# Value blocks of the later four heads are loaded at attention steps 5 and 8 instead of 2 and 5

## The chip, the cores and the metric

The kernel runs on one core of a Trainium2 chip. The metric is the device time of one execution in microseconds, lower is better.

## The reference

Two blocks follow each other: a sparse attention over a window and over block summaries, and a low-rank token mix with a two-layer network behind it. There are 4 batches, 8 heads, 768 tokens and a head size of 64; the network is 512 to 2048 to 512 wide.

```python
k_sum = k.reshape(B, H, nb, block, D).max(axis=3)      # block = 32
v_sum = v.reshape(B, H, nb, block, D).mean(axis=3)
scores_l = scale * q @ k.T                             # kept where |i - j| < 16
scores_s = scale * einsum(q, k_sum) + log(block)
a = softmax(concat([masked scores_l, scores_s]))
x = a @ concat([v, v_sum])                             # then heads side by side
u = x + (x.T @ U @ V).T
out = u + relu(u @ w_ch1) @ w_ch2
```

The change concerns `v_sum`: the mean of each block of 32 value rows, which the attention needs beside the values.

## The kernel before

Matmul operands are split into a high and a low part (ScalarE rounds, VectorE or POOL subtracts), so that each product takes three passes. The first batch's network also makes the split weights and stores the unsplit ones and some of their sums to DRAM. For each of the batches 2 to 4 (`cur`) two phases follow in the loop at the end of `body`:

- the **up phase** (`up_phase`), with the weights in eight groups of four blocks; it yields after every product of six matmuls (a *piece*), 54 pieces in the loop;
- the **down phase** (`down_phase`), sixteen blocks of weights.

Beside these matmuls, the attention of the next batch (`ahead`) is worked off in 32 steps of `later_step`. Step i belongs to head i // 3. The first 15 steps (0 to 14, `FIRST_STEPS`) are spread evenly over the pieces 4 to 54 of the up phase, so that step 2 stands at piece 10, step 4 at 17, step 5 at 20, step 7 at 27, step 8 at 30 and step 10 at 37. The others go into the down phase. So the up phase of batch 2 carries the first half of batch 3's attention, and the up phase of batch 3 that of batch 4.

Each engine works in the order in which the program is written out. Several orders matter here.

- **SyncE issues all DMAs.** Among them are the weights kept in DRAM (`whole`, in `fetch_weight`, called by `tick` four pieces after a block is used up by its split), keys `kt`, queries `qz`, values `vt`, the turned squares of the attention weights (`there`, then `at`), the outputs (`out_t`) and the value blocks (`stage`, from `vn`).
- **Weights.** `prepare` splits a fetched block: ScalarE casts the high part (L186), POOL subtracts (L187).
- **Value sums.** `load_vsum(st, g, i)` loads two blocks of 128 x 512 floats, 256 KB each, for half i of head group g (g = 1 are the later four heads). `add_vsum(st, g, i)` is a generator of seven or eight small POOL adds, put on a list `slow`; `drip` takes one of them per piece. After the second half POOL scales the sum (L275), and `value_summaries` (L340) copies it on ScalarE behind each head's values. For g = 1 the first such copy is that of step 16, at the beginning of the down phase.
- **Bank copies.** The product `third` of the up phase ends in a ScalarE copy (L1262), after which TensorE may use the bank again.

The blocks `stage`, the outputs `o` and some temporaries take turns in one pool of eight buffers.

Of the kernel before, what the change touches and what calls it, by code (L numbers as in the profile page):

```python
# [86 lines left out]
def body(ctx: ExitStack, tc, q0, q1, k, v, vn, uv, w1, w2, mask, ident, rep, out):  # L87
# [29 lines left out]
    def hidden_place(k, dt=F32):  # L117
        return wt.tile([P, 4 * NH], dt, name="place", tag=f"h{k}")
# [98 lines left out]
    def load_qk(st, h):  # L217
        load_k(st, h)
        load_q(st, h)
# [7 lines left out]
    def load_v(st, h):  # L227
        vt = kv.tile([KC, 2, NU, DV], F32, name="vt")
        nc.sync.dma_start(out=vt[:W, 0], in_=v[st.b, 0, :, h])
        nc.sync.dma_start(out=vt[NB:, 1], in_=v[st.b, 1, :, h])  # L230
        st.vt[h] = [vt[:, i] for i in range(2)]
# [7 lines left out]
    def load_vsum(st, g, i):  # L239

        parts = 2
        n = BLOCK * D // (2 * parts)
        spare = None
        if st.b == 1 or st.b == 2 and g == 0:
            spare = hidden_place(2 + i)
        st.vn[g, i] = []
        for j in range(parts):
            if spare is not None:
                t = spare[:, j * n : (j + 1) * n]
            else:  # L250
                t = mo.tile([P, DM], F32, name="stage", tag="val", bufs=VALS)[:, :n]
            k = i * parts + j
            nc.sync.dma_start(out=t, in_=vn[st.b, g, :, k * n : (k + 1) * n])
            st.vn[g, i].append(t)

    def add_vsum(st, g, i):

        for j, t in enumerate(st.vn.pop((g, i))):
            n = t.shape[1] // 2
            while n > D:  # L260
                nc.gpsimd.tensor_tensor(t[:, :n], t[:, :n], t[:, n : 2 * n], ALU.add)
                yield
                n //= 2
            if i == 0 and j == 0:
                st.vsum[g] = small.tile([P, DV], F32, name="vsum")
                nc.gpsimd.memset(st.vsum[g][:, D:], 1.0)
                nc.gpsimd.tensor_tensor(st.vsum[g][:, :D], t[:, :D], t[:, D : 2 * D], ALU.add)
                yield
            else:
                nc.gpsimd.tensor_tensor(t[:, :D], t[:, :D], t[:, D : 2 * D], ALU.add)  # L270
                yield
                nc.gpsimd.tensor_tensor(st.vsum[g][:, :D], st.vsum[g][:, :D], t[:, :D], ALU.add)
                yield
        if i == 1:
            nc.gpsimd.tensor_scalar_mul(st.vsum[g][:, :D], st.vsum[g][:, :D], 1.0 / BLOCK)  # L275
# [33 lines left out]
    def key_maxima(st, h):  # L309
        block_maxima(st, h)  # L310

        spread_maxima(st, h, nc.scalar.copy if st.b == 1 else nc.vector.tensor_copy)
# [25 lines left out]
    def value_summaries(st, h, i, copy):  # L338
        r0, r = 32 * (h % 4), (W, 0)[i]
        copy(  # L340
            st.vt[h][i][r : r + NB],
            st.vsum[h // 4][r0 : r0 + NB].unsqueeze(1).broadcast_to([NB, NU, DV]),
        )
# [19 lines left out]
    def scores_by_subtiles(st, h):  # L363

        st.neg[h] = small.tile([P, NU], F32, name="neg")
        qt, kt = st.qt[h].rearrange("p u q -> p (u q)"), st.kt[h]
        ps = [bank("ps_s") for _ in range(2)]  # L370
        for i in range(3):
            for s in range(2):
                for a in range(2):
                    j = ORDER.index(2 * i + a)
                    q0, k0 = 64 + j * P + 64 * s, (j // 2) * KP + (j % 2) * KC
                    r, c = 64 * ((s + a) % 2), 64 * s
                    nc.tensor.matmul(  # L377
                        ps[a][c : c + 64, i * KC : (i + 1) * KC],
                        qt[r : r + 64, q0 : q0 + 64],
                        kt[r : r + 64, k0 : k0 + KC],  # L380
                        start=True,
                        stop=True,
                        tile_position=(r, c),
                    )
        for a in range(2):
            st.ps_s[h, a] = ps[a]
# [5 lines left out]
    def exponentials(st, h, a):  # L392
        ps = st.ps_s.pop((h, a))
        if h not in st.e and st.b == 0:
            st.e[h] = e0[h % 4]
        elif h not in st.e:
            st.e[h] = att.tile([P, NU * KC + PAD], F32, name="e", bufs=1)
            if st.b > 1:
                nc.gpsimd.memset(st.e[h][:, NU * KC :], 0.0)
        e = tiles_of(st.e[h])  # L400
        for i, u in enumerate(tiles_in_bank(st, a)):
            m = 0 if u == 0 else (3 if u == NU - 1 else 1 + u % 2)
            nc.vector.tensor_tensor_reduce(  # L403
                out=e[:, u, :],
                in0=ps[:, i * KC : (i + 1) * KC],
                in1=mask_sb[:, m, :],
                scale=-SCALE,
                scalar=BIG,
                op0=ALU.add,
                op1=ALU.min,  # L410
                accum_out=st.neg[h][:, u : u + 1],
            )
            nc.scalar.activation(  # L413
                e[:, u, :],
                e[:, u, :],
                AF.Exp,
                bias=st.neg[h][:, u : u + 1],
                scale=-1.0,
            )
# [16 lines left out]
    def send_squares(st, h):  # L436
        there = dram.tile([P, 4, NU * 32], F32, name="there")
        nc.sync.dma_start(out=there, in_=st.at[h].rearrange("p j u q -> p j (u q)"))
        st.at[h] = there

    def fetch_squares(st, h):

        there = st.at[h].rearrange("(i k) j c -> j k i c", k=32)
        at = st.at[h] = att.tile([P, 4, NU, 32], F32, name="at", tag="at", bufs=1)
        for j in range(4):
            nc.sync.dma_start(
                out=at[32 * j : 32 * j + 32].rearrange("k i u q -> k i (u q)"), in_=there[j]
            )
# [39 lines left out]
    def square_values(st, h):  # L488

        at, vt = st.at.pop(h), st.vt[h]  # L490
        ps = st.psx[h] = bank("ps_x")
        for u in range(NU):
            for i in range(4):
                nc.tensor.matmul(  # L494
                    ps[32 * i : 32 * i + 32, u * DV : (u + 1) * DV],
                    at[:KC, i, u],
                    vt[u % 2][:, (u // 2) * 2 + (i // 2 + u) % 2],
                    start=True,
                    stop=True,
                    tile_position=(0, 32 * i),  # L500
                )

    def normalise(st, h):
        ps = st.psx.pop(h)[:, : NU * DV].rearrange("p (u d) -> p u d", d=DV)
        s = small.tile([P, NU], F32, name="sum")
        nc.vector.tensor_scalar_add(s, ps[:, :, D], 1e-9)
        nc.vector.reciprocal(s, s)
        nc.vector.tensor_tensor(
            st.x[:, :, h * D : (h + 1) * D],
            ps[:, :, :D],  # L510
            s.unsqueeze(2).broadcast_to([P, NU, D]),
            ALU.mult,
        )
# [19 lines left out]
    slow = []  # L533
# [10 lines left out]
    def later_step(st, i):  # L544

        h, a = divmod(i, 3)
        if a == 0:  # L550
            if 1 <= h <= H:
                send_squares(st, h - 1)
            if 2 <= h <= H + 1:
                fetch_squares(st, h - 2)
            if h < H:
                scores_by_subtiles(st, h)
                exponentials(st, h, 0)
            if 3 <= h <= H:
                load_v(st, h - 1)
        elif a == 1:  # L560
            if h < H:
                exponentials(st, h, 1)
            if h + 1 < H:
                key_maxima(st, h + 1)
            if 1 <= h <= H:
                for t in range(2):
                    value_summaries(st, h - 1, t, nc.scalar.copy)
        else:
            if h + 2 < H:
                load_qk(st, h + 2)  # L570
            if h == 2:
                st.x = mo.tile([P, NU, DM], F32, name="x")
            if 2 <= h <= H + 1:
                square_values(st, h - 2)
                normalise(st, h - 2)
            if h < H:
                turn_squares(st, h)
        if i in (2, 5):
            load_vsum(st, 1, i // 5)
        if i in (4, 7):  # L580
            slow.append(add_vsum(st, 1, i // 7))
        if i in MIX:
            mix(st, 2 * MIX.index(i))
        if i - 1 in MIX:
            mix_back(st, 2 * MIX.index(i - 1))
# [389 lines left out]
    st = sts[0]  # L975
# [465 lines left out]
```

## Time and profile before

| | |
|---|---|
| timed runs of before | 666.3, 666.86, 669.9 us; median 666.86 |
| profiled execution | 668.33 us, of it the span 666.5 us |
| mean granted TensorE clock | 0.997 |
| busy: VectorE, ScalarE, POOL | 371.7, 358.5, 361.0 us |
| up phase of batch 2 / 3 / 4 | from about 226 / 381 / 532 us |
| down phase of batch 2 / 3 / 4 | from about 298 / 449 / 595 us |
| DMA: read from HBM, written | 91.10 MB, 24.12 MB |

Lines of the profile name an engine, the source line, the operation and the tiles that it writes and reads. In the timeline the first two columns are the start and the duration in us, and the bracket at the end is the idle time ahead of it with what ended that. Rows of a list of waits give the total, the number and the longest. Rows on DMAs give the size of one and the us from issue to landing.

### The profile page before, as it was taken

The numbers are of one execution on the slowest core, as the hardware profiler recorded it, in microseconds if no ns is written. First come the engines' busy times: TensorE is split into PE (matmuls) and PEld (weight loads), VectorE is DVE, ScalarE is ACT, GpSimd is POOL, SyncE is SP. The second block draws the span as 40 slices with busy tenths as digits, with TensorE's granted clock in tenths as the row PEclk, the third lists the DMA queues.
The fourth block names the chain that finished last, engine by engine and source line by source line (L and its number), as shares of the span: only waits on it lengthen the run. The fifth ranks groups of instructions, "written<-read, shape, count | busy, mean of one in ns | idle before, by whom it ended". The sixth has DMA issues, their size and how long they took to land.

```text
span 666.5 us, 14015 instructions
## 1 busy us (share of the span) xinstructions
PE 640.6 (96%) x5232; PEld 562.6 (84%) x5232; DVE 371.7 (56%) x1006; ACT 358.5 (54%) x803; POOL 361.0 (54%) x402
## 2 busy tenths in 40 slices
PE   5899999999999898999999999999999999999997
PEld 4789889988888797997787899997787899998885
DVE  5578866668777763567544645566644521232223
ACT  4666666655553555765453467665453365553322
POOL 5424975965577676762336487662334375653310
PEclk9999999999999998999999999999999999999999
DMA  8997497766774268787457059787441055331002
GB/s 219 228 367 239 135 315 240 230 173 195 227 225 163 72 178 265 213 251 203 147 142 205 25 171 325 228 247 204 138 143 59 24 171 178 112 126 64 32 1 94
DMA packets 76420, 116.13 MB, mean 174 GB/s; under 512 B 6976, under 2 KB 52928, under 8 KB 76352
## 3 DMA queue, kind: packets, MB, share of 16 engines
q1 hardware_dynamic: 76352, 115.24, 57.1%
q8 instruction: 41, 0.67, 0.4%
q14 instruction: 27, 0.22, 0.1%
HBM read 91.10 MB, written 24.12 MB: 173 GB/s over the span
## 4 chain that ended last, share of the span: by engine, by line
PE 83%; DVE 4%; DMA 4%; ACT 3%; POOL 2%; issue 2%; SPq 1%; ACTq 0%; POOLq 0%; DVEq 0%
PE acc L1288 30%; PE ps_h L1203 25%; PE acc L942 7%; PE ps_h L920 7%; PE ps_x L494 3%; PE ps_s L354 2%; PE ps_o L739 2%; PE ps_s L377 2%; DMA place<-in_uv 1%; DMA place<-in_q 1%; PE ps_m L666 1%; DMA whole<-up 1%; PE ps_t L463 1%; PE ps_x L480 1%; POOL place L187 1%
## 5 line engine op out<-in xcount | busy, mean ns | idle before, releaser
L187 POOL TENSOR_TENSOR parts<-whole,parts 128x512 fp32r<-128x512 f32 (+1 forms) x144 | 180.5, 1262 | 160.4 <-ACT parts L186 151.3
L1288 PE MATMUL acc<-parts,gh 128*128 128x512 f32 x576 | 192.3, 399 | 0.0
L1203 PE MATMUL ps_h<-op,parts 128*128 128x384 f32 x1008 | 187.5, 340 | 3.2 <-ACT place L1262 2.9
L1203 PEld LDWEIGHTS ps_h<-op,parts 128*128 128x128 f32 x1008 | 175.4, 189 | 6.2 <-ACT place L1262 3.2
L1288 PEld LDWEIGHTS acc<-parts,gh 128*128 128x128 f32 x576 | 108.1, 188 | 23.7 <-issue 1.7
L1288 PE MATMUL acc<-parts,gl 128*128 128x512 f32 x288 | 112.6, 391 | 0.0
L1273 DVE SCALAR_TENSOR_TENSOR gl<-place,gh 128x768 fp32r<-128x768 f32 x48 | 56.2, 1171 | 97.1 <-ACT gh L1272 97.1
L186 ACT CAST parts<-whole 128x512 fp32r<-128x512 f32 (+1 forms) x144 | 83.6, 584 | 9.9 <-DMA whole<-up 8.2
L920 PE MATMUL ps_h<-place 128*128 128x384 f32 x384 | 74.5, 342 | 0.0
L1272 ACT ACTIVATE gh<-place 128x768 fp32r<-128x768 f32 x48 | 40.6, 846 | 60.0 <-PE acc L1288 59.9
L413 ACT ACTIVATE e<-e,neg 128x120 f32<-128x120 f32 x144 | 46.3, 386 | 47.4 <-DVE neg L403 45.7
L942 PE MATMUL acc<-place,gh 128*128 128x512 f32 x192 | 68.4, 410 | 1.3 <-POOL place L187 1.3
L920 PEld LDWEIGHTS ps_h<-place 128*128 128x128 f32 x384 | 65.9, 188 | 1.0 <-DVE place L721 0.3
L162 POOL TENSOR_SCALAR val<-place 128x512 f32<-128x512 f32 (+1 forms) x30 | 47.0, 1582 | 30.8 <-ACT place L149 14.2
L1288 PEld LDWEIGHTS acc<-parts,gl 128*128 128x128 f32 x288 | 54.2, 188 | 9.9 <-DVE gl L1273 0.3
L187 POOL TENSOR_TENSOR place<-val,place 128x512 fp32r<-128x512 f32 x29 | 39.4, 1378 | 18.6 <-ACT place L186 15.3
L187 POOL TENSOR_TENSOR op<-tmp,op 128x384 fp32r<-128x384 f32 x24 | 25.4, 1067 | 39.2 <-ACT op L186 39.2
L942 PEld LDWEIGHTS acc<-place,gh 128*128 128x128 f32 x192 | 35.6, 188 | 10.5 <-POOL place L187 3.2
L403 DVE CUSTOM_DVE_ANT_0 e<-ps_s,mask_sb 128x120 f32<-128x120 f32 x144 | 32.5, 276 | 13.3 <-PE ps_s L377 8.5
L942 PE MATMUL acc<-place,gl 128*128 128x512 f32 x96 | 37.6, 392 | 0.0
L932 ACT ACTIVATE gh<-ps_h 128x384 fp32r<-128x384 f32 x32 | 15.7, 490 | 36.4 <-PE ps_h L920 36.0
L1263 DVE TENSOR_TENSOR place<-place,ps_h 128x384 f32<-128x384 f32 x24 | 13.3, 553 | 38.4 <-ACT place L1262 38.3
(124 smaller groups left out, 858.8 us busy)
## 6 DMA issues: line engine op xcount, KB each, us to landing
place<-in_w SPq DMA_DIRECT2D x32, 512.0 KB, 5.6
whole<-up SPq DMA_DIRECT2D x24, 512.0 KB, 3.9
whole<-down SPq DMA_DIRECT2D x24, 512.0 KB, 3.7
whole<-up SPq DMA_DIRECT2D x24, 384.0 KB, 3.3
vt<-in_v SPq DMA_DIRECT2D x48, 146.2 KB, 4.1
kt<-in_k SPq DMA_DIRECT2D x24, 288.0 KB, 5.4
out_t<-o SPq DMA_DIRECT2D x32, 192.0 KB, 2.2
there<-squares SPq DMA_DIRECT2D x16, 384.0 KB, 4.4
```

The costliest lines, as they stand in the source:

```text
L162: nc.gpsimd.tensor_scalar(f32(bits), f32(hi), 0.0, None, ALU.mult)
L186: nc.scalar.copy(hi, val)
L187: engine.tensor_tensor(lo, val, f32(hi), ALU.subtract)
L403: nc.vector.tensor_tensor_reduce(out=e[:, u, :], in0=ps[:, i * KC : (i + 1) * KC], in1=mask_sb[:, m, :], scale=-SCALE, scalar=BIG, op0=ALU ...
L413: nc.scalar.activation(e[:, u, :], e[:, u, :], AF.Exp, bias=st.neg[h][:, u : u + 1], scale=-1.0,)
L494: nc.tensor.matmul(ps[32 * i : 32 * i + 32, u * DV : (u + 1) * DV], at[:KC, i, u], vt[u % 2][:, (u // 2) * 2 + (i // 2 + u) % 2], start=Tr ...
L920: nc.tensor.matmul(ps[:, :NH], w_split[0, f][:, c % 2, part_w, c // 2], ut[:, c, :], start=(n == 0), stop=(n == 3 * NC - 1),)
L942: nc.tensor.matmul(acc[t], gt[:, sl], w_split[1, f][:, part_w], start=(first and j == 0), stop=(last and j == 2),)
L1203: nc.tensor.matmul(ps, a[:, sa, i], b[:, sb, i], start=(first and n == 0), stop=(n == 5), skip_group_check=not first,)
L1272: nc.scalar.activation(gh, h, AF.Relu)
L1273: nc.vector.scalar_tensor_tensor(gl, h, 0.0, f32(gh), ALU.max, ALU.subtract)
L1288: nc.tensor.matmul(acc[t], gt[:, sl], w[:, part_w], start=(f == 0 and j == 0), stop=(f == NF - 1 and j == 2),)
```

## The change

In `later_step`, the loads of the later four heads' value blocks go from the steps 2 and 5 to the steps 5 and 8, and the adds from the steps 4 and 7 to the steps 7 and 10.

```diff
-        if i in (2, 5):
-            load_vsum(st, 1, i // 5)
-        if i in (4, 7):
-            slow.append(add_vsum(st, 1, i // 7))
+        if i in (5, 8):
+            load_vsum(st, 1, i // 8)
+        if i in (7, 10):
+            slow.append(add_vsum(st, 1, i // 10))
```

TensorE, VectorE and ScalarE keep their order. On SyncE, this is the place of step 2 in the up phase of batch 2: keys, queries, value blocks, then kept weights (`whole`), the turned squares, and weights again. Before:

```order
L208 DMA kt<-in_k 128x3x192
L214 DMA qz_84<-in_q 64x3x128
L215 DMA qz_84<-in_q 64x4x128
L253 DMA stage<-in_vn 128x512 x2
L877 DMA whole<-up_109 128x768
L438 DMA there<-squares 128x768
L877 DMA whole<-up_110 128x1024
```

And now:

```order
L208 DMA kt<-in_k 128x3x192
L214 DMA qz_84<-in_q 64x3x128
L215 DMA qz_84<-in_q 64x4x128
L877 DMA whole<-up_109 128x768
L438 DMA there<-squares 128x768
L877 DMA whole<-up_110 128x1024
```

The two value blocks no longer stand between the queries and the weights. Step 5 has two value blocks in both orders. The other place on SyncE is step 8 of the same up phase; here the difference, with the fetches of the turned squares (`at`) at its end:

```order
 L214 DMA qz_84<-in_q 64x3x128
 L215 DMA qz_84<-in_q 64x4x128
+L253 DMA stage<-in_vn 128x512 x2
 L877 DMA whole<-up_112 128x768
 L438 DMA there<-squares 128x768
```

Two value blocks now stand ahead of the weights and the squares of that step. The up phase of batch 3 has the same two differences; there an output (`out_t`) stood between the value blocks and the weights at step 2.

On POOL, the first adds (L261 to L272) of the up phase of batch 2 stood among the splits of weights (L187) like this before:

```order
L187 TENSOR_TENSOR parts<-whole,parts 128x2x256 x2
L261 TENSOR_TENSOR stage<-stage 128x256
L187 TENSOR_TENSOR parts<-whole,parts 128x256
L261 TENSOR_TENSOR stage<-stage 128x128
L187 TENSOR_TENSOR parts<-whole,parts 128x2x256
L266 MEMSET vsum 128x1
L267 TENSOR_TENSOR vsum<-stage 128x64
```

And now, from the same first row on:

```order
L187 TENSOR_TENSOR parts<-whole,parts 128x2x256 x2
L187 TENSOR_TENSOR parts<-whole,parts 128x256
L187 TENSOR_TENSOR parts<-whole,parts 128x2x256 x3
L399 MEMSET e 128x8
L187 TENSOR_TENSOR parts<-whole,parts 128x256
L187 TENSOR_TENSOR parts<-whole,parts 128x2x256
L261 TENSOR_TENSOR stage<-stage 128x256
L261 TENSOR_TENSOR stage<-stage 128x128
```

Six splits now come ahead of the first add; the scaling of the finished sum (L275) stands five splits later than before.

## The prediction

> **What bounds the kernel now.** I began with the page's first table: TensorE is the bound, so a change pays only where it removes idle or slow time of that engine.
>
> ```profile
> PE 640.6 (96%) x5232; PEld 562.6 (84%) x5232; DVE 371.7 (56%) x1006; ACT 358.5 (54%) x803; POOL 361.0 (54%) x402
> ```
>
> Next the waits of TensorE inside the two stretches that the change touches. The first list is from 223 to 381 us (batch 2 in its up phase, batch 3 in attention), the second from 381 to 533 us (batches 3 and 4).
>
> ```profile
> PE ps_h L1203 <- ACT place L1262: 2.9, 1, 2.9
> ...
> PE ps_h L1203 <- POOL parts L187: 0.3, 1, 0.3
> ```
>
> So there is one wait of size after the start, of 2.87 us, and all but none in the second up phase. The timeline of TensorE shows where it lies, and that the 24 matmuls behind it take longer than the 24 of a later piece.
>
> ```profile
> 246.50 6.54 PE L1203 MATMUL ps_h<-op,parts 128*128 128x384 f32 x36
> 255.92 6.02 PE L1203 MATMUL ps_h<-op,parts 128*128 128x384 f32 x24 [2.87 <-ACT place L1262]
> 269.93 4.45 PE L1203 MATMUL ps_h<-op,parts 128*128 128x384 f32 x24
> ```
>
> Idle runs from 253.05 to 255.92. Then 24 matmuls take 6.02 us and not 4.45, which is 1.57 us more. The windows say why: in 256 to 261 us the granted clock was 0.66, which is 5 x 0.34 = 1.70 us lost. (In the rows below, the columns behind the window are its length, then busy time of PE, PEld, DVE, ACT and POOL, the granted clock, the DMA share and GB/s.)
>
> ```profile
> 250.00:253.00 3.00, 3.00 (x18) 2.72 (x16) 1.33 (x8) 0.06 (x1) 0.26 (x1) 1.00 1.02 404
> 253.00:256.00 3.00, 0.13 (x2) 0.09 (x1) 0.10 (x1) 2.96 (x8) 1.94 (x2) 1.00 1.10 340
> 256.00:261.00 5.00, 5.00 (x20) 5.00 (x21) 1.99 (x4) 2.60 (x7) 4.54 (x8) 0.66 0.85 256
> ```
>
> I take 1.6 us, between the two readings. The place costs 2.87 + 1.6 = 4.5 us in this execution. What ended the wait stands on ScalarE:
>
> ```profile
> 248.26 0.61 ACT L186 CAST parts<-whole 128x512 fp32r<-128x512 f32 x1
> 252.94 0.62 ACT L186 CAST parts<-whole 128x512 fp32r<-128x512 f32 x1 [4.06 <-DMA whole<-up]
> 253.46 0.96 ACT L413 ACTIVATE e<-e,neg 128x120 f32<-128x120 f32 x3
> 254.45 1.05 ACT L340 COPY vt<-vsum 24x390 f32<-24x390 f32 x2
> 255.40 0.46 ACT L1262 COPY place<-ps_h 128x384 f32<-128x384 f32 x1
> ```
>
> ScalarE stood for 4.06 us on the landing of one block of kept up weights. Three exponentials, two summary copies and the copy of L1262, for which TensorE waits, are queued behind that cast. From the landing (252.86) to TensorE's restart pass 3.06 us, so a landing by 253.05 - 3.06 = 249.99 would cost TensorE nothing. SyncE's issues show what that block queued behind; the second fence gives, for the issues at 243.99, 244.64, 245.28 (the pair's second) and 245.81, the us to landing in the last column.
>
> ```profile
> 243.99 0.60 SPq L215 DMA_DIRECT2D qz<-in_q  x1
> 244.64 1.08 SPq L253 DMA_DIRECT2D stage<-in_vn  x2
> 245.81 0.38 SPq L877 DMA_DIRECT2D whole<-up  x1
> ```
>
> ```profile
> qz<-in_q SPq DMA_DIRECT2D x1, 128.0 KB, 3.6
> stage<-in_vn SPq DMA_DIRECT2D x1, 256.0 KB, 5.0
> 245.28 0.43 SPq L253 DMA_DIRECT2D stage<-in_vn  x1
> stage<-in_vn SPq DMA_DIRECT2D x1, 256.0 KB, 5.8
> whole<-up SPq DMA_DIRECT2D x1, 384.0 KB, 7.0
> ```
>
> The queries landed at about 247.6, the value blocks at 249.6 and 251.1, the weights at 252.86. The two value blocks (512 KB) stand just ahead of the weights, and they are what the change takes from there.
>
> **The change, part by part.** No instruction is added or removed; two DMA issues and 7 to 9 small POOL adds move, once per value half, twice per batch, in the up phases of batches 2 and 3.
>
> *The first pair of loads leaves step 2.* The weights are then issued at 244.64 instead of 245.81, in the first value block's place. That block landed 5.0 us after this issue. The weights carry 128 KB more, 0.3 us at the 404 GB/s of the row 250 to 253, so they land by 244.64 + 5.0 + 0.3 = 249.95. The early end: behind the queries (247.6) with 384 KB at 404 GB/s (0.97 us) gives 248.6. I take 249.7, near the late end, since that is what a block in this place did. The limit is 249.99, so the wait goes, with 0.3 us in hand, and the clock loss goes with it. Is ScalarE late for another reason? The last row maximum that its exponentials need is ready at 250.08:
>
> ```profile
> 250.00 0.08 DVE L403 DVE_READ_ACCUMULATOR2_ANT neg<- 128x1 f32 x1
> ```
>
> From there follow one exponential (0.32), the copies (1.05) and L1262 (0.46): 251.9, over a microsecond ahead of 253.05. So only the landing can hold TensorE there. Bounds for this term: 4.5 us gone at most, and 2.9 at least (first rival).
>
> The next batch is a second witness. There the pair stands one issue further ahead of the same weights, and no wait of TensorE results:
>
> ```profile
> 399.06 0.38 SPq L877 DMA_DIRECT2D whole<-up  x1
> whole<-up SPq DMA_DIRECT2D x1, 384.0 KB, 6.1
> 405.15 0.62 ACT L186 CAST parts<-whole 128x512 fp32r<-128x512 f32 x1 [0.26 <-DMA whole<-up]
> 401.70 2.35 PE L1203 MATMUL ps_h<-op,parts 128*128 128x384 f32 x12
> 404.13 8.58 PE L1203 MATMUL ps_h<-op,parts 128*128 128x384 f32 x48
> ```
>
> The 37th matmul of this up piece, which needs the same L1262, begins about 404.13 + 24 x 0.18 = 408.4. A landing 3.3 us ahead sufficed there; the one I expect, 3.35 ahead of 253.05, is alike. It also says that the later weight loads keep up when TensorE does not pause, with a value pair still at step 5 as now. In batch 3's up phase the change therefore gains nothing: 0.
>
> *Step 5 keeps a pair* (the first, no longer the second). Its queue has 512 KB less ahead of it.
>
> *Step 8 gets a pair*, behind the queries issued at 267.18. The next weights are issued only at 271.78, since they wait for POOL:
>
> ```profile
> 267.18 0.60 SPq L215 DMA_DIRECT2D qz<-in_q  x1
> qz<-in_q SPq DMA_DIRECT2D x1, 128.0 KB, 4.8
> 271.78 0.33 SPq L877 DMA_DIRECT2D whole<-up  x1
> 272.68 2.21 SPq L446 DMA_DIRECT2D at<-there  x4
> 281.56 0.89 PE L494 MATMUL ps_x<-vt,at 120*32 120x65 f32 x48
> DMA to landing us min/median/max: 3.7/4.4/5.0
> ```
>
> Two issues (1.08 us) fit into the 4 us that SyncE stands there, so nothing is issued later. The pair's transfer, 1.3 us at 404 GB/s or 3.5 us (from 247.6 to 251.1, over which the old pair landed), is over by 275.5, since those queries landed 4.8 us after their issue, at 272.0. The first to feel it are the four fetches of the turned squares: issued until 274.9, landed by 279.3, needed by TensorE at 281.56, with 2.3 us to spare. Cost: 0. If that cover is gone it is the last rival.
>
> *The adds on POOL.* They run two groups later, beside other splits. POOL was busy 19.0 of 24 us in the old stretch and 7.85 of 14 in the one behind it, which takes the second group:
>
> ```profile
> 254.00:278.00 24.00, 22.08 (x197) 20.92 (x197) 10.62 (x37) 15.27 (x38) 19.00 (x30) 0.93 0.77 220
> 278.00:292.00 14.00, 14.00 (x143) 13.25 (x143) 7.95 (x35) 9.50 (x23) 7.85 (x8) 1.00 0.87 245
> 277.50 0.37 POOL L275 TENSOR_SCALAR vsum<-vsum 128x64 f32<-128x64 f32 x1
> 303.93 1.05 ACT L340 COPY vt<-vsum 24x390 f32<-24x390 f32 x2
> ```
>
> The sum is ready at 277.87 and first used at 303.93. Ten pieces later (six matmuls each, 6.54/6 = 1.1 us, and some attention between) it is ready near 290: over 10 us in hand. Splits wait on a single add of at most 0.73 us at a time, as now. Cost: 0, bounds -0.3 (a split freed earlier near 255) and +0.3.
>
> **Sum.** 668.33 (span 666.5 and 1.83 around it) - 4.5 = **663.8 us**. The median of the timed runs of before, 666.86, lies 1.5 under the profiled execution. Either two of three timed runs had the wait without the slow clock (668.33 - 1.6 = 666.7 fits two of them); then they fall by 2.9, to 663.4 to 664.0. Or they had both, and end at 661.8 to 662.4. I give the first reading six parts in ten, so that 663.8 is the forecast, 0.46% under the median. What a measurement of this kernel can tell from no change is about 0.5%, 663.5 us: the forecast sits at this edge.
>
> On the clock: the gap of 2.87 us was followed by a granted clock of 0.66 in the next window, while after the gap of 1.29 us below 12 matmuls took 2.35 us, as they do at 401.70 without a gap. [...]
>
> ```profile
> 230.88 0.44 PE L963 MATMUL ps_o<-ident_sb,r 128*128 128x128 f32 x2 [1.29 <-DVE r L955]
> 231.07 2.35 PE L1203 MATMUL ps_h<-op,parts 128*128 128x384 f32 x12
> ```
>
> **The rivals.** *Half of the wait stays.* If the pair costs the queue only its bytes at the best rate seen, 512 KB at 404 GB/s = 1.3 us, the weights land at 251.56 and TensorE waits 1.57 us, with no slow clock (as after 1.29). Gain 1.3 + 1.6: **665.4**. For it: 250 to 253 did run at 404 GB/s. Against it: the old pair's landings follow the one before them by 2.0 and 1.5 us. [...]
>
> *The wait moves.* TensorE runs 4.5 us earlier from here on; if the next weights (issued at 246.76) or those behind step 5's pair now land late, the same chain on ScalarE stalls once, with or without the clock: **666.7 to 668.3**, no change. For it: ScalarE has a cast of those weights every few us. Against it: batch 3, where the same order ran without a pause.
>
> *Slower.* The place is step 8, in both up phases. The pair delays the four fetches, and TensorE waits in front of L494. It decides from 2.3 us of delay on. If it brought the old gap and the slow clock twice, the time would be 663.8 + 2 x 4.5 = **672.8**. For it: the pair may cost 3.5 us. Against it: all before it has landed by 272.0, when the next issue (271.78) has only begun, so that part of the 3.5 us falls into an empty queue.
>
> That the change does not do what it says I give nothing: the order of issues shows the pair gone from step 2.
>
> **How the numbers follow.** Forecast 0.70 (661.8 to 664.6), half the wait 0.12, moved wait 0.11, slower 0.07. The range 661.8 to 667.0 holds the forecast, the first rival and part of the second, some 85%. Below 663.5 lies the whole second reading and four tenths of the first, 0.64 of the forecast: faster 0.45. Within 0.5%: the rest of the forecast and both middle rivals, 0.48. Slower: 0.07.
>
> **What would show it.** Right: no wait of L1203 on L1262 of over 0.5 us near 253, a granted clock of 1.00 from 256 to 261, the weights behind step 2 landing near 249.7, down matmuls starting 4.5 us earlier. Wrong: a cast of weights that stands over 1 us for its landing in either up phase, a gap in front of L494 near 277 or 432, or a slow clock at any place behind 230. If timed runs of before prove to lack the slow clock, the gain is 2.9 and not 4.5.

## The result and the profile after

| | before | changed |
|---|---|---|
| median of six timed runs | 666.58 us (664.86 to 669.9) | 663.66 us (661.93 to 665.96) |
| ratio to before, 95% interval | | 0.9946 (0.9921 to 0.9972) |
| profiled execution, its span | 668.33, 666.5 us | 662.67, 660.9 us |
| first up phase: first matmul of L1203 to first of L1288 | 71.92 us | 67.32 us |
| second up phase, the same way | 67.52 us | 67.51 us |

The kernel is faster by 0.3 to 0.8%; the forecast was 663.8 us. The last two rows are the better measure here. They are stretches between two instructions of one trace, and all that lies ahead of the up phase, whose length differs from run to run (226.09 us before and 225.20 with the change, in these two profiles), is left out of them.

First, of the changed kernel, the waits of TensorE from 223 to 381 us, where 2.9 us on L1262 headed the list of before:

```profile
PE ps_o L963 <- DVE r L955: 1.3, 1, 1.3
PE ps_o L963 <- ACT r L955: 1.1, 1, 1.1
```

The wait on L1262 is gone; the two that remain were there before as well, ahead of the place. TensorE's timeline of the changed kernel shows the same matmuls as the rows "x36" and "x24 [2.87 ...]" of before, now in one piece:

```profile
245.62 10.82 PE L1203 MATMUL ps_h<-op,parts 128*128 128x384 f32 x60
```

Sixty matmuls in 10.82 us, without a gap and without a slow part; the 36 of before took 6.54 and the 24 behind the gap 6.02. The reason stands in the timeline of ScalarE of the changed kernel:

```profile
247.38 0.61 ACT L186 CAST parts<-whole 128x512 fp32r<-128x512 f32 x1
248.99 0.62 ACT L186 CAST parts<-whole 128x512 fp32r<-128x512 f32 x1 [0.99 <-DMA whole<-up]
249.52 0.96 ACT L413 ACTIVATE e<-e,neg 128x120 f32<-128x120 f32 x3
250.50 1.05 ACT L340 COPY vt<-vsum 24x390 f32<-24x390 f32 x2
251.46 0.46 ACT L1262 COPY place<-ps_h 128x384 f32<-128x384 f32 x1
```

SyncE's queue of the same kernel, in the timeline:

```profile
243.10 0.60 SPq L215 DMA_DIRECT2D qz<-in_q  x1
243.80 0.55 SPq L877 DMA_DIRECT2D whole<-up  x1
```

And its list of DMAs, for these two issues (last column: us to landing):

```profile
qz<-in_q SPq DMA_DIRECT2D x1, 128.0 KB, 4.9
whole<-up SPq DMA_DIRECT2D x1, 384.0 KB, 5.1
```

The weights follow the queries directly, land 5.1 us after their issue instead of 7.0, and ScalarE stands 0.99 us for them instead of 4.06. This whole kernel began its up phase 0.89 us earlier (225.20 against 226.09), so places are compared from the first matmul of L1203: the weights landed 26.77 us after it before, and 23.71 us now. TensorE needs them by 23.9 (253.05 - 3.06 - 226.09). Behind the place the clock stays up, in the windows of the changed kernel (behind the engines' busy times stand the granted clock, the share of the DMA engines and GB/s):

```profile
252.00:255.00 3.00, 3.00 (x18) 3.00 (x18) 1.96 (x3) 2.22 (x6) 2.03 (x2) 1.00 1.06 278
255.00:260.00 5.00, 5.00 (x49) 4.59 (x48) 1.81 (x8) 3.10 (x9) 3.18 (x4) 1.00 0.92 299
```

Both windows have a granted clock of 1.00, where before the one from 256 to 261 had 0.66.

### The profile page after: what moved, and what is told of

Same layout as the page of the kernel before. It is cut to its first block, busy times and chain, and to the rows that moved or that the text cites. A ratio compares the mean times of both kernels' runs of the same rounds, so it can differ in the third digit from the quotient of the medians.

```text
span 660.9 us, 14013 instructions
## 1 busy us (share of the span) xinstructions
PE 639.8 (97%) x5232; PEld 562.0 (85%) x5232; DVE 372.5 (56%) x1006; ACT 358.8 (54%) x803; POOL 361.8 (55%) x402
## 4 chain that ended last, share of the span: by engine, by line
PE 86%; DVE 4%; ACT 3%; POOL 2%; DMA 2%; SPq 1%; issue 1%; ACTq 0%; POOLq 0%; DVEq 0%
PE acc L1288 31%; PE ps_h L1203 26%; PE acc L942 8%; PE ps_h L920 6%; PE ps_x L494 3%; PE ps_s L354 2%; PE ps_o L739 2%; PE ps_s L377 2%; PE ps_t L463 1%; DMA place<-in_v 1%; PE ps_m L666 1%; PE ps_x L480 1%; PE ps_n L293 1%; POOL place L187 1%; POOL val L162 1%
## 5 line engine op out<-in xcount | busy, mean ns | idle before, releaser
L187 POOL TENSOR_TENSOR parts<-whole,parts 128x512 fp32r<-128x512 f32 (+1 forms) x144 | 180.8, 1265 | 156.0 <-ACT parts L186 147.4
L1288 PE MATMUL acc<-parts,gh 128*128 128x512 f32 x576 | 192.4, 399 | 0.0
L1203 PE MATMUL ps_h<-op,parts 128*128 128x384 f32 x1008 | 185.7, 338 | 0.4 <-POOL parts L187 0.4
L1203 PEld LDWEIGHTS ps_h<-op,parts 128*128 128x128 f32 x1008 | 173.9, 188 | 3.2 <-issue 1.0
L1288 PEld LDWEIGHTS acc<-parts,gh 128*128 128x128 f32 x576 | 108.1, 188 | 23.7 <-issue 1.7
L1288 PE MATMUL acc<-parts,gl 128*128 128x512 f32 x288 | 112.6, 391 | 0.0
L1288 PEld LDWEIGHTS acc<-parts,gl 128*128 128x128 f32 x288 | 54.2, 188 | 9.8 <-DVE gl L1273 0.3
L187 POOL TENSOR_TENSOR place<-val,place 128x512 fp32r<-128x512 f32 x29 | 39.9, 1395 | 18.3 <-ACT place L186 18.3
L187 POOL TENSOR_TENSOR op<-tmp,op 128x384 fp32r<-128x384 f32 x24 | 25.4, 1067 | 39.2 <-ACT op L186 39.2
```

The source lines that it names most:

```text
L187: engine.tensor_tensor(lo, val, f32(hi), ALU.subtract)
L1203: nc.tensor.matmul(ps, a[:, sa, i], b[:, sb, i], start=(first and n == 0), stop=(n == 5), skip_group_check=not first,)
L1288: nc.tensor.matmul(acc[t], gt[:, sl], w[:, part_w], start=(f == 0 and j == 0), stop=(f == NF - 1 and j == 2),)
```

## The experiments

The theory: the pair of value blocks in SyncE's queue ahead of one block of weights held ScalarE, and through it TensorE, and part of the time was the slow clock behind that gap. Its rivals: the moved adds on POOL, a gain in the second up phase, any load this early, or a lucky profile. All kernels below keep every other line of the kernel. The diffs show the lines that matter, and `...` stands where lines are left out; the adds are at steps 7 and 10 where nothing else is said. "Stretch" is the up phase measured as in the table; "landing" is that of the 384 KB weights behind step 2, from the first matmul of L1203 on.

**Only the adds move.**

```diff
-        if i in (4, 7):
-            slow.append(add_vsum(st, 1, i // 7))
+        if i in (7, 10):
+            slow.append(add_vsum(st, 1, i // 10))
```

> Only the adds move (steps 7 and 10); the four loads stay at steps 2 and 5. Measured on the stretch of the first up phase, from its first matmul of L1203 to the first of L1288: 71.93 us before, 67.32 with the change. Theory (the two value blocks ahead of the weights in SyncE's queue make the wait): nothing gained, the wait of L1203 on L1262 stays at 2.4 to 3.3 us near 253, the stretch is 70.2 (without a slow clock behind) to 72.3, time as before within 0.4%. Rival (the adds, by leaving POOL free for a split near 255, make the gain): wait gone, stretch 67.3, time 0.5% less.

Measured: ratio 1.0019 (0.9995 to 1.0043), landing 26.29, stretches 69.89 and 67.50. TensorE's timeline of this kernel:

```profile
257.02 4.46 PE L1203 MATMUL ps_h<-op,parts 128*128 128x384 f32 x24 [2.40 <-ACT place L1262]
```

And its window behind the gap:

```profile
257.00:262.00 5.00, 4.98 (x48) 4.73 (x48) 2.55 (x4) 3.27 (x7) 3.53 (x4) 1.00 0.93 284
```

The wait stays, so the adds have no part in the gain. But here the 24 matmuls behind it took 4.46 us at a clock of 1.00: a wait of the expected size, without the slow clock. The stretch is therefore 0.3 us below its range.

**The change for one batch alone**, first for batch 3 and then, with the two entries exchanged, for batch 4.

```diff
...
+        loads, adds = (((5, 8), (7, 10)), ((2, 5), (4, 7)))[st.b - 2]
+        if i in loads:
+            load_vsum(st, 1, loads.index(i))
+        slow.extend(add_vsum(st, 1, adds.index(j)) for j in adds if i == j)
```

> The change for batch 3 alone (loads and adds in the first up phase); batch 4 as before. Theory: the whole gain, the first up phase 67.3 +/- 0.3 with no wait on L1262, the second 67.5 +/- 0.3 as in both kernels, time as with the change, ratio to before 0.992 to 0.997. Rival (part of the gain comes from the second up phase): second up phase longer than 67.8, time 1 us or more above the changed kernel.

> The change for batch 4 alone (the second up phase); batch 3 as before. Theory: no gain, wait of 2.4 to 3.3 us on L1262 near 253 stays, first up phase 70.2 to 72.3, second 67.5 +/- 0.3. Rival (the second up phase gains too): second up phase under 67.2.

Measured: with batch 3 alone the ratio is 0.9955 (0.9937 to 0.9973), the stretches 67.20 and 68.23. With batch 4 alone one execution gave 668.61 us, a wait of 2.81, stretches of 71.85 and 67.51. So the gain lies in the first up phase, as forecast. But with batch 3 alone the second stretch lies above its range of 67.2 to 67.8, so the pair in its old place is not quite free there. The timeline of that kernel shows it:

```profile
405.58 2.70 PE L1203 MATMUL ps_h<-op,parts 128*128 128x384 f32 x14 [0.46 <-ACT place L1262]
```

There the weights landed 24.71 us after that phase's first matmul; in the profile of before it was 23.86, against the same limit of about 23.9. The old place in batch 4 cost nothing in one execution and 0.46 us in another, so part of the rival holds, as 0 to 0.7 us of the stretch.

**One block of the pair at step 2.**

```diff
...
+        half = {2: (0,), 5: (1,)} if st.b == 2 else {}
+        if i in (5, 8, *half):
+            load_vsum(st, 1, i // 8, half.get(i, (0, 1)))
...
```

> As the changed kernel, but in the first up phase one of the two value blocks is loaded at step 2 as before (256 KB ahead of the weights), the other at step 5. Theory (the wait is the queue's length, some 1.5 us a block, and the limit has 0.2 us in hand): the weights land 25.0 to 25.6 us after the first matmul of L1203 (26.77 before, 23.71 with the change), TensorE waits 1.0 to 1.6 us on L1262, and with a gap as short as 1.29 us the clock stays at 1.00: stretch 68.3 to 69.0. Rival A (the block costs only its bytes, 0.6 us): wait 0.3 to 0.5, stretch 67.7. Rival B (the clock is lost for any gap of over 1 us here): stretch about 70.2.

Measured: landing 25.09, stretch 68.68, and no slow clock:

```profile
253.87 4.44 PE L1203 MATMUL ps_h<-op,parts 128*128 128x384 f32 x24 [1.21 <-ACT place L1262]
```

One block costs 1.4 us of landing and 1.2 us of wait, as expected, and this gap cost no clock. In the second up phase, which is that of the changed kernel, a new wait stood in front of L494 of step 8 (this stretch was 68.41):

```profile
417.17 0.89 PE L494 MATMUL ps_x<-vt,at 120*32 120x65 f32 x48 [0.85 <-DMA at<-there]
```

These are the fetches of step 6, which stand behind the pair of step 5 in both kernels. It is what the prediction's last rival named, at another step.

**The pair one step later, behind those weights.**

```diff
-        if i in (5, 8):
-            load_vsum(st, 1, i // 8)
+        if i in (3, 5):
+            load_vsum(st, 1, i // 5)
```

> The adds and the second pair's load follow the changed kernel's order of adds, but the pairs are loaded at steps 3 and 5: in SyncE's order the first pair then stands behind the 384 KB weights (which it stood ahead of before) and ahead of the next 512 KB. Theory (what counts is only which transfer stands behind the pair, and how much time that one has): the 384 KB weights land 23.5 to 23.9 us after the first matmul of L1203 as with the change, the next block 29 us (26.5 with the change), ScalarE then stands 1.5 to 2.5 us for that one, and TensorE waits 0 to 1.0 us: stretch of the first up phase 67.3 to 68.4, clock 1.00. Rival (any pair this early costs the same 2.9 us, wherever it stands among these issues): wait of 2.4 us and more, stretch 69.9 to 72.

Measured: landing 23.90, stretches 67.48 and 67.51, 663.55 us in one execution. The next weights landed 27.98 us after the first matmul, 1.5 later than with the change where 2.5 were expected, and ScalarE stood 0.41 us for them where 1.5 to 2.5 were:

```profile
253.80 0.62 ACT L186 CAST parts<-whole 128x512 fp32r<-128x512 f32 x1 [0.41 <-DMA whole<-up]
```

The pair may stay as early as step 3, if it stands behind the one transfer that has no time in hand. What counted here was what it is ahead of, not the step.

**All four blocks at step 2**, in the first up phase.

```diff
...
+        for j in range(2):
+            if i == ((2, 2) if st.b == 2 else (5, 8))[j]:
+                load_vsum(st, 1, j)
...
```

> First up phase: all four value blocks (1 MB) at step 2 ahead of the 384 KB weights, none at steps 5 and 8; second up phase as changed. Theory (1.5 us of queue a block): landing 29.3 to 30.3 us after the first matmul of L1203, TensorE waits 5.4 to 6.4 us on L1262, the clock is halved behind it, 1.7 to 2.9 us more: stretch 74.4 to 76.6. Rival A (512 KB at 404 GB/s more, 1.3 us): landing 28.1, wait 4.2, stretch about 73.2. Rival B (a longer gap costs no more clock than none): stretch 67.3 plus the wait alone.

Measured: landing 27.42, stretch 71.01. ScalarE and TensorE in the timeline of this kernel:

```profile
253.20 0.62 ACT L186 CAST parts<-whole 128x512 fp32r<-128x512 f32 x1 [4.71 <-DMA whole<-up]
256.18 4.46 PE L1203 MATMUL ps_h<-op,parts 128*128 128x384 f32 x24 [3.52 <-ACT place L1262]
```

And its window behind the gap:

```profile
258.00:263.00 5.00, 5.00 (x49) 4.59 (x48) 1.58 (x8) 2.77 (x8) 3.26 (x4) 1.00 0.91 263
```

Two expectations fell. Twice the bytes cost 27.42 - 26.58 = 0.8 us more (26.58 is the mean of the five landings with one pair), not 3; and the longest gap of all was followed by no slow clock. For the first, the throughput (last column) in two windows ahead of the landing, of this kernel:

```profile
247.00:249.00 2.00, 2.00 (x13) 2.00 (x12) 0.47 (x2) 1.49 (x5) 0.43 (x1) 1.00 0.85 251
249.00:252.00 3.00, 3.00 (x20) 3.00 (x19) 1.94 (x13) 0.00 (x0) 0.86 (x1) 1.00 0.83 296
```

And the same two windows of before:

```profile
247.00:249.00 2.00, 2.00 (x13) 2.00 (x12) 0.40 (x5) 1.85 (x5) 0.04 (x1) 1.00 0.52 88
249.00:252.00 3.00, 3.00 (x19) 3.00 (x18) 2.33 (x13) 0.00 (x0) 1.26 (x1) 1.00 0.99 357
```

Before, the queue moved 88 GB/s for two microseconds in which the pair was in it, though more was queued, and 357 GB/s in the three behind them. With four blocks it moved 251 and 296 GB/s. So more bytes went through in the same five microseconds, which is how the second pair could cost 0.8 us, less than its 1.3 us at 404 GB/s. In the five executions with one pair here, the two microseconds from 20.9 us after the first matmul of L1203 ran at 83 to 196 GB/s, and the weights landed at 26.7 to 26.8 where it was 83 to 103, and at 26.4 and 26.3 where it was 178 and 196. A slow stretch is thus a part of the first pair's price, but even the fastest of the five landed 2.6 us later than with the change. What makes the queue slow there was not tried and stays open.

**Both pairs at step 5.**

```diff
...
+        for j in range(2):
+            if i == 5:
+                load_vsum(st, 1, j)
...
```

> Both pairs (1 MB) at step 5 in both up phases, none at steps 2 and 8; adds as changed. Behind them stand 512 KB of weights and the four fetches of step 6, which in the changed kernel's profile had 0.5 us (weights, ScalarE) and 1.6 and 0.5 us (fetches, TensorE's L494, first and second up phase) in hand. Theory (a pair costs what stands behind it some 3 us): ScalarE stands 2 to 3 us for those weights, and TensorE waits 1.0 to 2.0 us in the first and 2.0 to 3.0 us in the second up phase, in front of L494 or of a product of L1203: stretches 68.3 to 71.5 and 69.5 to 72. Rival (the place at step 2 is a special one, others have room): both stretches under 67.9.

Measured: stretches 68.22 and 68.69, 665.77 us in one execution, and these waits in the two up phases:

```profile
265.18 0.89 PE L494 MATMUL ps_x<-vt,at 120*32 120x65 f32 x48 [0.96 <-DMA at<-there]
417.13 0.89 PE L494 MATMUL ps_x<-vt,at 120*32 120x65 f32 x48 [1.12 <-DMA at<-there]
```

The wait is where it was expected but smaller, as is that of ScalarE for the weights behind the pairs (1.1 and 1.6 us, where 2 to 3 were expected), and the stretches lie 0.1 and 0.8 us below their ranges; the rival's, under 67.9 in both, is missed too. With 1.6 and 0.5 us in hand, the second pair delayed the fetches by 2.5 and 1.6 us. The place at step 2 is not a special one: here, too, a pair ahead of fetches with little time in hand made a wait, of 0.96 and 1.12 us.

**Steps 6 and 8**, a version without a pair ahead of either tight place.

```diff
-        if i in (5, 8):
+        if i in (6, 8):
...
-        if i in (7, 10):
+        if i in (8, 10):
```

> A version meant to be better: pairs at steps 6 and 8, adds at 8 and 10, so that neither the weights of step 2 nor the fetches of step 6 stand behind a pair. Theory: no wait of TensorE of over 0.4 us in either up phase, fetches of step 6 landing over 2 us ahead of L494 in both; stretches 67.2 to 67.5 and 67.4 to 67.6, time as with the change within its noise, ratio to before 0.991 to 0.998. Rival (what a pair delays at its new place, 384 KB of weights, holds ScalarE): wait on a product of L1203 of over 0.5 us behind step 6, time up to 2 us above the changed kernel.

Measured: ratio 0.9941 (0.9906 to 0.9976), stretches 67.70 and 67.51, no wait of over 0.4 us apart from the 1.3 us on L963 that every kernel has. The first stretch is 0.2 us above its range; the weights behind step 2 landed 0.2 us past the limit of 23.9. That is the changed kernel's time within the noise; it does not beat it.

**The two kernels once more.** The half clock had come behind gaps of 2.87 and 2.81 us, and not behind 2.40 and 3.52. So the kernel before was profiled twice more, and the changed one once, without an edit.

> The kernel before, unchanged, for another profile. So far the clock records change at times that lie whole multiples of 3.413 us apart, and the gap on L1262 was followed by half a clock where one such interval held 2.3 or 2.8 us of it, and by none where the fullest held 1.7 or 1.85. Theory (what counts is the idle share of one interval of this grid, and the grid lies anywhere): wait 2.3 to 3.0 us; a half clock for 3.41 us follows if an interval holds 2.2 us or more of it, and none if none holds over 1.9. Stretch of the first up phase 69.6 to 70.3 without, 71.4 to 72.0 with. Rival (the length of the gap decides: 2.8 and more lose the clock, 2.4 does not): loss whenever the wait is 2.8 or more, wherever the grid lies.

> The kernel before, unchanged, for a third profile. As for the second one: wait 2.3 to 3.0 us; half clock behind it if one interval of the grid holds 2.2 us or more of the gap (stretch 71.4 to 72.0), none if no interval holds over 1.9 (69.6 to 70.3). Rival: the length of the gap alone decides.

> The changed kernel, unchanged, for another profile. Theory: no wait on L1262 of over 0.5 us near 253, first up phase 67.2 to 67.8, second 67.5 to 68.5, where up to 0.9 us in front of L494 of step 8 may come and go (the fetches behind step 5's pair had 0.46 us in hand in one profile). Rival (the first profile of it was a lucky one): a wait of over 1 us on L1262, first up phase 68.3 or more.

Measured: of before, stretches 71.85 and 71.58 (second up phases 67.61 and 67.65), landings 26.70 and 26.44; of the changed kernel 67.54 and 67.55, landing 23.92, no wait on L1262. TensorE's timeline of the second profile of before, and the window behind the gap:

```profile
257.24 6.01 PE L1203 MATMUL ps_h<-op,parts 128*128 128x384 f32 x24 [2.81 <-ACT place L1262]
```

```profile
258.00:261.40 3.40, 3.40 (x13) 3.40 (x12) 1.39 (x2) 1.40 (x4) 3.32 (x7) 0.50 0.72 218
```

The same two views of the third profile of before:

```profile
257.27 6.01 PE L1203 MATMUL ps_h<-op,parts 128*128 128x384 f32 x24 [2.55 <-ACT place L1262]
```

```profile
258.50:261.90 3.40, 3.40 (x13) 3.40 (x12) 0.93 (x2) 1.48 (x3) 3.29 (x7) 0.50 0.89 297
```

A gap of 2.55 us lost the clock and one of 3.52 us did not, so length alone did not decide, and the rival falls. The section on the hardware takes it up.

## Why the prediction was right

- **The bound, and the one wait.** Right. In both traces TensorE is the bound. The profiled execution is 5.66 us shorter: 4.60 of that (71.92 - 67.32) lie between the first matmul of L1203 and the first of L1288, where 4.5 were forecast, 0.89 ahead of the up phase, where the change moves nothing, and 0.2 elsewhere.
- **The landing.** Forecast 249.7 with 0.3 us in hand, which is 23.6 us after the first matmul; measured 23.71 (23.92 in the second profile). It is as tight as was said: the limit is 23.9, and the version with steps 6 and 8 landed at 24.11 with 0.2 us of wait.
- **The slow clock as part of the price.** Right for the profile (1.6), but it belongs to the gap only in some executions: in four of five with the old place, not in the one with the moved adds. The mean of the five stretches is 71.42, against 67.43 for the two of the changed kernel: 4.0 us, 0.6%, inside the interval of the ratio. That interval is wide, though: a gain of 2.9 us, the wait without the slow clock, lies in it as well.
- **The second up phase: 0.** Right in the profiles (67.52 and 67.51). Of the five executions with the old place there, one was 0.7 us longer (0.46 of it the wait shown above); the other four, 67.50 to 67.65, are like four of the new order, 67.51 to 67.62, which also had one long one, 68.41 with its wait on the fetches. The forecast took one quiet execution as a witness.
- **The adds: 0.** Right; alone they change nothing (1.0019).
- **Step 8: 0.** Right; no wait stood in front of L494 of step 11 in any profile of the changed order. One sign that the prediction had named as wrong did appear, a cast that stands over 1 us for its weights: 1.2 us at 386.15 in the second up phase. TensorE did not wait for it, and the kernel before has the like (1.3 us at 391.71), so that sign was too strict. The last rival named a place with more room than that behind step 5, where 0.46 us were in hand. It does not tell the kernels apart, since both have a pair there.
- **What was wrong beside the sum.** The reading that two of three timed runs of before had no slow clock, held for six parts in ten, has little left: four of five profiles had it. The mean granted clocks of the timed runs point the same way. A mean of 0.999 or more leaves no room for the 1.7 us of one such stretch; 4 of 29 runs of before had it, and 13 of 22 runs of the three kernels that keep the pair away from that place (the changed one, batch 3 alone, steps 6 and 8). The 1.5 us between the profiled execution and the median are of the size by which executions differ in reaching the up phase at all: the first matmul of L1203 stood between 225.20 and 228.77 us in the thirteen profiles. So the nearness of 663.8 to 663.66 is partly luck; the 4.5 us of the stretch is what was predicted well.
- **The first rival** (a pair costs its bytes at 404 GB/s) is wrong for the first pair, whose landing cost 2.9 us and not 1.3, and too high for a second one behind it, which cost 0.8.

## What to carry to other kernels

A load that nobody waits for can still cost time, as here (a wait of 2.87 us), through what stands behind it in the queue: look for the transfer on whose landing an engine stood, and read the issues just ahead of it. Then move what is least urgent behind that transfer; one place was enough here (23.90 us to the landing with the pair at step 3), and the step in itself did not matter, only what stands behind the load there. Where executions differ by more than the gain, measure between two instructions around the place, and look at several traces before a cost that comes and goes, such as a slow clock, is counted in full.

## What the runs showed of the hardware

**In these runs the half clock followed an idle share, not a length.** In the traces here, the times at which the granted clock changes lie multiples of 3.413 us from one another: in that of before it is 1.00 until 257.05, 0.50 until 260.46 (one interval) and 1.00 again for 406.19 us (119 intervals). Each half clock behind the place lasted one such interval and began at the end of the one in which most of the gap lay: before, the gap from 253.05 to 255.92 has 2.28 us in the interval from 253.64 to 257.05. Laid on this grid, the gaps on L1262 in front of L1203 read:

| kernel | gap, us | most of it in one interval, us | half clock behind it |
|---|---|---|---|
| before | 2.87 | 2.28 | yes |
| batch 4 alone | 2.81 | 2.81 | yes |
| before, second profile | 2.81 | 2.66 | yes |
| before, third profile | 2.55 | 2.17 | yes |
| all four blocks at step 2 | 3.52 | 1.85 | no |
| only the adds | 2.40 | 1.71 | no |
| one block at step 2 | 1.21 | 1.16 | no |

In this up phase, the clock was kept behind up to 1.85 idle microseconds of an interval of 3.41, and lost behind 2.17 and more. The bounds expected ahead of the last two profiles, 1.9 and 2.2, held for the second one of before (2.66) and left its third (2.17) open. Where the grid lies differs between executions: in the three profiles of before, the half clock began at 257.05, 258.0 and 258.5 us, and the gap had ended at 255.92, 257.24 and 257.27. Gaps of 2.55 to 2.87 us cost 1.6 us more, and one of 3.52 us did not.

**A queue of DMAs ran slowly in stretches while more was queued.** Behind the queries of step 2 the rate fell to 88 GB/s for 2 us before the change, and to 112 for 1 us with it; behind that it was 357 before and 361 with the change. The second row of the changed kernel is the stretch behind it:

```profile
245.20:246.20 1.00, 1.00 (x23) 0.84 (x16) 0.46 (x5) 0.28 (x2) 0.34 (x2) 1.00 0.76 112
246.20:249.00 2.80, 2.80 (x18) 2.80 (x17) 1.20 (x10) 1.80 (x6) 0.93 (x1) 1.00 0.95 361
```

So the price of the transfers in this queue was not their size over a rate: the first 256 KB cost 1.4 us, the first 512 KB 2.9, and the first megabyte 3.7, where executions with the same order ahead of these weights differ by up to 0.6 us (they landed at 23.50 to 24.11 in the six with the pair gone from step 2 and nothing else in its place). SyncE's own time is in these prices: it issued the weights 0.65, 1.1 and 2.1 us later. How much of a price is that, and how much is bytes, was not separated.
